# Operand forms of a two-level product moved from VectorE to GpSimd and to an earlier product, in a kernel of attention, Fourier mixing and a channel MLP

## The chip, the core and the metric

The kernel runs on one core of a Trainium2 chip. The metric is the device time of one execution in microseconds (us). The core's engines run side by side, each through its own queue in program order: TensorE (PE; its weight loads are listed apart as PEld), VectorE (DVE), ScalarE (ACT), GpSimd (POOL) and SyncE (SP), which starts the DMA transfers here. They wait for each other by semaphores.

## What is computed

```
# 8 batches, 8 heads, 576 rows, head dimension 64; all fp32
scores = (q @ k.T) / sqrt(64)
scores = where(scores >= max(scores) - tau, scores, -1e9)
attn   = exp(scores - max(scores)); attn = attn / (sum(attn) + 1e-9)
x      = attn @ v                                # heads side by side: (8, 576, 512)
u      = x + real(fft(fft(x, axis=1), axis=2))   # Fourier mixing
un     = (u - mean(u)) / sqrt(var(u) + 1e-6)     # over the 512 channels
out    = u + relu(un @ w_ch1) @ w_ch2            # 512 -> 2048 -> 512
```

## The kernel before

**Steps.** Attention runs in 160 steps, 20 for each batch: four pairs of heads, five steps for each pair. A step computes scores (L440, L446), takes their row maxima on VectorE (L520), exponentials on ScalarE (L526), the threshold and masked sum (L530, L540), the reciprocal of the sum (L385, L388) and the scaling (L549). The result is transposed on TensorE (`pw`, L605; its end rows `pe`, L587) and copied out by ScalarE (L607, L609; `ends`, L593), and is multiplied by the values (`pv`, L636).

**Mixing.** The 576 rows of a batch are folded by symmetry into `f` (L687, L692, L699, L703), one pair of heads at a time; `partial_sums` (L729, L730, then L721 three times, by way of `scaled`) makes sums of the folded halves as soon as enough pairs are there, and `mixing` takes them up in the next batch (L751 to L754 and again L721). Then come small matrix products along the rows (`py`, L766, copied out by ScalarE as `y_e` and `y_o`, L771 and L776) and along the channels (`pa`, L783 and L787; L799 on ScalarE, L803 and L804 on VectorE, L808 and L812 on GpSimd). A row is normalised (`pn`, L858; L863, L864; statistics L869, L870).

**Channel MLP.** The 4608 rows of all batches go through the MLP in groups of 512, group 0 in the plain way and groups 1 to 8 in `two_level`. There each of the two matrix products is made with seven products of half-size blocks in place of eight (a Strassen-Winograd scheme). For the second product this is done on two levels. On the outer level, h (the hidden activations, four quarters a11, a12, a21, a22 in the tile `hs`) gives seven left operands: a11, a12, S1 = a21 + a22, a22, S2 = S1 - a11, a11 - a21 and a12 - S2, numbered 1, 2, 5, 4, 6, 7, 3 in the order in which they are used. I call the seven products by their place in this order, 0 to 6. On the inner level each operand gives seven inner blocks, of which four must be formed: `l2_forms` (L1191) makes two on VectorE and two on GpSimd, of 128x512 each, during the product before. Seven inner products `jn` of four matmuls each (L1398) make up one outer product.

**Rooms.** S1 lies in `s1_tile`. The operands S2, a11 - a21 and a12 - S2 are formed in place by `l1_form` (L1168), each in four pieces of 128x512. S2 is written over S1 before the change; so its pieces stand behind TensorE's reading of S1 in product 2. The room of a11 has had its last reader once a11 - a21 is formed (product 1) and S1 - a11 (products 2 and 3).

**Side jobs.** Which job is issued after which inner product is written out by hand: `at_slots(at, slots, jobs)` (L1321 to L1342) puts jobs at (outer product, inner product), and `slot` (called after the matmuls of each inner product) issues them, so they take their place in the queue of their engine there. Besides operand forms these are the sums over the inner products for each output quarter: `gather` (L1263, five additions on GpSimd) and `finish` (L895, two operations on VectorE, which scale by the row's standard deviation and add to u; L890 takes the reciprocal before the first of them). What is not done within `two_level` goes on in the first product of the next group. The results of the seven products go from PSUM into rows of `w_all`, by ScalarE (L1410) or added by VectorE (L1412, L1418).

**How the two are woven.** `two_level` is a generator that yields after each inner product; `fill` (L1487) advances it within the steps of attention by a budget, and `mix(1)` advances the mixing. TensorE's order is thus the order of the program text. The first products of group 3 run beside the last steps (18 and 19) of a batch and the first of the next. Groups 6 to 8 run with hardly any attention beside them; group 8 is the last (`whole`), where outer products 5 and 6 are plain (L1377).

A next group's first product takes row blocks of the normalised u as its right operand, formed by GpSimd (`t_room`, L1132) in groups 1 to 6 and by VectorE in the last two; its results are taken up by VectorE (L1147) and ScalarE (L1152).

## Time and profile before

| | us |
|---|---|
| median of 3 runs | 1551.99 |
| lowest and highest | 1551.36, 1552.12 |
| profiled execution | 1552.55 |
| its span in the profile | 1550.8 |
| TensorE busy (of the span) | 1523.1 |
| VectorE busy | 1066.9 |
| ScalarE busy | 917.1 |
| GpSimd busy | 776.8 |

The page also gives the granted TensorE clock, 0.999 as a mean. Of the operations that the change touches, the trace has these:

| operation | line | engine | count | median ns of one |
|---|---|---|---|---|
| S2, in four pieces for each group | L1168 | VectorE | 32 | 684 |
| a11 - a21 | L1168 | GpSimd | 32 | 1277 |
| a12 - S2 | L1168 | GpSimd | 32 | 1341 |
| `scaled` of f | L721 | VectorE | 24 | 531 |
| `scaled` of the sums | L721 | VectorE | 8 | 528 |
| `finish` from `w_all` | L895 | VectorE | 64 | 478 |

The outer products of group 3 begin at 778.1, 790.9, 800.1, 810.9, 822.8, 835.1 and 850.6 us of the span. In the windows between them, from product 2 on, VectorE is busy for 10.12, 9.59, 12.16, 11.26 and 9.34 us (the last up to 869.5) and GpSimd for 6.18, 3.97, 7.87, 5.01 and 10.53 us.

A line of the timeline gives the start, the busy time, the engine, the line, the operation, the tile written and those read, shapes, and how many instructions it stands for; in brackets stands how long the engine was idle before it and who ended that. "Busy" is the time from the first to the last of the instructions in the line. In the list of groups, "mean ns" is of one instruction.

### The profile page before, as it was taken

How to read it: one execution, taken by the hardware profiler on the slowest of the kernel's cores; microseconds unless marked ns; L12 is line 12 of the kernel's file. 1: busy time of each engine (PE TensorE's matmuls, PEld its weight loads, DVE VectorE, ACT ScalarE, POOL GpSimd, SP SyncE). 2: the span in 40 equal slices, each digit the busy share in tenths (PEclk: the TensorE clock that was granted, in tenths of full speed). 3: DMA queues.
4: the chain of work that ended last, by engine and by line, in shares of the span. 5: the costliest groups of instructions: out<-in, count | busy, mean ns of one | idle time of the engine just before them, and what ended most of it. 6: DMA issues, size and time to landing. Idle time of an engine off the chain costs nothing.

```text
span 1550.8 us, 27036 instructions
## 1 busy us (share of the span) xinstructions
PE 1523.1 (98%) x9786; PEld 1185.1 (76%) x9786; DVE 1066.9 (69%) x2141; ACT 917.1 (59%) x1921; POOL 776.8 (50%) x964
## 2 busy tenths in 40 slices
PE   8999999999999999999999999999999999999999
PEld 5555555556788777877788778887788778989999
DVE  7987676846779466866588566956687666746546
ACT  6875675655656576656766666666666676232131
POOL 3775553034365643545254724555264626646635
PEclk9999999999999999999999999999999999999999
DMA  6423233465866344634464354635464534646655
GB/s 168 132 59 119 78 92 108 136 204 159 269 200 189 111 150 133 195 102 141 143 186 140 117 159 135 195 93 166 125 191 135 159 117 140 221 163 226 236 198 184
DMA packets 248907, 239.31 MB, mean 154 GB/s; under 512 B 197027, under 2 KB 218533, under 8 KB 228678
## 3 DMA queue, kind: packets, MB, share of 16 engines
q1 hardware_dynamic: 246262, 237.28, 50.1%
q8 instruction: 78, 1.28, 0.3%
q10 hardware_dynamic: 2512, 0.30, 0.1%
q14 instruction: 55, 0.45, 0.1%
HBM read 205.93 MB, written 31.46 MB: 153 GB/s over the span
## 4 chain that ended last, share of the span: by engine, by line
PE 84%; DVE 9%; ACT 3%; DMA 1%; POOL 1%; issue 1%; SPq 0%; ACTq 0%; DVEq 0%; POOLq 0%
PE ph L1210 25%; PE po L1398 18%; PE sc L440 9%; PE pv L636 9%; PE pw L605 7%; PE po L933 4%; PE ph L909 2%; PE sc L446 2%; PE py L766 2%; PE pa L783 1%; PE pe L587 1%; PE pa L787 1%; PE pm L360 1%; PE po L1377 1%; PE pn L858 1%
## 5 line engine op out<-in xcount | busy, mean ns | idle before, releaser
L520 DVE TENSOR_REDUCE neg<-sc 128x1 f32<-128x576 f32 x216 | 154.2, 750 | 113.0 <-PE sc L440 99.6
L526 ACT ACTIVATE e<-sc,neg 128x576 f32<-128x576 f32 x216 | 158.6, 734 | 121.6 <-DVE neg L520 121.5
L1147 DVE TENSOR_TENSOR hs<-ph,hs 128x512 f32<-128x512 f32 (+1 forms) x128 | 105.4, 823 | 168.0 <-PE ph L1210 97.7
L1398 PE MATMUL po<-w,w_all 128*128 128x128 f32 x1728 | 219.4, 276 | 0.3 <-ACT ends L593 0.3
L1398 PEld LDWEIGHTS po<-w,w_all 128*128 128x128 f32 x1728 | 205.0, 192 | 9.4 <-issue 4.0
L1156 POOL TENSOR_TENSOR w<-hs 128x512 f32<-128x512 f32 x32 | 42.1, 1317 | 313.8 <-ACT hs L1152 240.0
L540 DVE SCALAR_TENSOR_TENSOR e<-sc,thr,e 128x576 f32<-128x576 f32 x216 | 168.3, 812 | 20.6 <-ACT thr L530 20.6
L1210 PE MATMUL ph<-u_t,w 128*128 128x256 f32 x768 | 180.9, 382 | 0.5 <-DMA w<-f 0.5
L440 PE MATMUL sc<-kT,qT 64*128 64x288 f32 x1024 | 169.8, 431 | 7.1 <-DVE e L477 6.1
L607 ACT COPY e_t<-pw 128x512 f32<-128x512 f32 x256 | 148.6, 595 | 44.1 <-PE pw L605 42.7
L605 PE MATMUL pw<-ident,e 128*128 128x128 f32 x1152 | 168.8, 273 | 6.0 <-ACT ends L593 1.9
L549 ACT ACTIVATE e<-e,den 128x576 f32<-128x576 f32 x216 | 157.4, 775 | 8.9 <-DVE den L388 8.2
L1210 PEld LDWEIGHTS ph<-u_t,w 128*128 128x128 f32 x768 | 140.9, 190 | 23.6 <-issue 5.3
L1210 PE MATMUL ph<-w_all,w 128*128 128x256 f32 x672 | 157.1, 382 | 1.1 <-DVE w_all L1132 1.0
L605 PEld LDWEIGHTS pw<-ident,e 128*128 128x128 f32 x1152 | 134.8, 141 | 21.9 <-issue 5.6
L1152 ACT ACTIVATE hs<-hs 128x512 f32<-128x512 f32 (+1 forms) x96 | 74.1, 772 | 114.5 <-DVE hs L1147 113.7
L1210 PEld LDWEIGHTS ph<-w_all,w 128*128 128x128 f32 x672 | 123.4, 190 | 23.9 <-issue 4.9
L440 PEld LDWEIGHTS sc<-kT,qT 64*128 64x128 f32 x1024 | 96.3, 187 | 57.1 <-issue 23.7
L1263 POOL TENSOR_TENSOR w_all<-w_all 128x128 f32<-128x128 f32 (+2 forms) x160 | 118.4, 757 | 29.1 <-DVE w_all L1418 20.2
L1398 PE MATMUL po<-w,hs 128*128 128x128 f32 x912 | 120.0, 278 | 0.3 <-ACT ends L593 0.3
L1398 PEld LDWEIGHTS po<-w,hs 128*128 128x128 f32 x912 | 109.9, 192 | 9.9 <-issue 8.0
L593 ACT COPY ends<-pe 128x128 f32<-128x128 f32 (+1 forms) x128 | 38.1, 298 | 58.7 <-PE pe L587 40.1
(227 smaller groups left out, 2945.3 us busy)
## 6 DMA issues: line engine op xcount, KB each, us to landing
w<-f SPq DMA_DIRECT2D x150, 1024.0 KB, 4.9
hs<-in_moe_w_ch_dram SPq DMA_DIRECT2D x23, 512.0 KB, 4.7
q_in<-in_q_dram SPq DMA_DIRECT2D x128, 72.0 KB, 4.3
out_dram<-u SPq DMA_DIRECT2D x36, 256.0 KB, 2.5
k_in<-in_k_dram SPq DMA_DIRECT2D x124, 72.0 KB, 2.4
v_in<-in_v_dram SPq DMA_DIRECT2D x64, 128.0 KB, 5.0
f<-w SPq DMA_DIRECT2D x14, 512.0 KB, 3.3
f<-w SPq DMA_DIRECT2D x7, 1024.0 KB, 4.8
```

What stands on the lines that cost most here:

```text
L440: nc.tensor.matmul(sc[j][:, c, 0:HALF], qT[hp, 128 * t : 128 * t + 128], kT[hp, k0 + HALF * c : k0 + HALF * (c + 1)], start=True, stop=True,)
L520: nc.vector.tensor_reduce(out=neg[:, j : j + 1], in_=sc[j][:, :, 0:HALF], axis=AXIS_XY, op=ALU.max, negate=True,)
L526: nc.scalar.activation(out=ej, in_=sc[j][:, :, 0:HALF], func=ACT.Exp, bias=neg[:, j : j + 1], scale=1.0)
L540: nc.vector.scalar_tensor_tensor(out=ej, in0=sc[j][:, :, 0:HALF], scalar=thr[:, j : j + 1], in1=ej, op0=ALU.is_ge, op1=ALU.mult, accum_out ...
L549: nc.scalar.activation(out=e[:, S * j : S * (j + 1)], in_=e[:, S * j : S * (j + 1)], func=ACT.Copy, scale=den[:, j : j + 1],)
L605: nc.tensor.transpose(pw[:, c, :], e[:, c0 : c0 + 128], ident[:, :])
L607: nc.scalar.copy(e_t[:, 4 * j : 4 * j + 4, qs], pw[:, :, :])
L636: nc.tensor.matmul(pv[64 * j : 64 * j + 64, 0:m], vt[:, 2 * c + j, :], e_t[:, 4 * j + c, 0:m] if c < 4 else ends[:, 0, 0:m], start=(c == 0 ...
L1147: nc.vector.tensor_tensor(out=to, in0=bank, in1=to if other is None else other, op=ALU.add)
L1210: nc.tensor.matmul(bank[:, 256 * q : 256 * q + 256].rearrange("p (two n) -> p two n", two=2), left[:, 256 * c + 128 * q : 256 * c + 128 * ...
L1263: return lambda: eng.tensor_tensor(out=to, in0=to, in1=other, op=ALU.add)
L1398: nc.tensor.matmul(to, lefts[m][j][:, s], right_[:, 128 * s : 128 * (s + 1)], start=jn in (0, 4) and s == 0, stop=s == 3, skip_group_check ...
```

## The change

1. S2 goes into the room of a11 instead of S1's, and GpSimd forms its four pieces in product 2 (after inner products 0, 1, 2 and 4). VectorE did so before, at the end of product 2 and the start of 3.
2. a12 - S2 (operand 3) is formed by GpSimd in product 3 instead of product 4.
3. The gather and the finish of the first output quarter, from `v_11`, move: the gather from product 2 to product 5, the finish from product 4 to product 6, after inner products 3 and 5. In the last group they go to product 4.
4. `partial_sums` starts earlier: L729 and L730 are issued at the end of step 18 instead of in step 19. The L721 of the sums stays in step 19 and the two L721 of f come in step 19 as well, where they came in the first step of the next batch. The last `next(partials)` after the loop goes.

The matmuls, their order and the order in which DMAs are issued are the same.

```diff
-        a = {1: a11, 2: a12, 5: s1_tile[:, :], 4: a22, 6: s1_tile[:, :], 7: a21, 3: a12}
+        a = {1: a11, 2: a12, 5: s1_tile[:, :], 4: a22, 6: a11, 7: a21, 3: a12}
...
         at_slots(1, (1, 2, 4, 6), l1_form(a21, a11, a21, (P, P, P, P)))
-        at_slots(2, (4, 5, 6), l1_form(s1_tile, s1_tile, a11, (V, V, V, V))[0:3])
-        at_slots(3, (0,), l1_form(s1_tile, s1_tile, a11, (V, V, V, V))[3:4])
-        at_slots(4, (1, 2, 4, 6), l1_form(a12, a12, s1_tile, (P, P, P, P)))
-        at_slots(2, (0, 1, 2, 3, 4), gather(P, v_11))
-        at_slots(4, (2, 4), [lambda n=n: finish(0, 0, v_11)[n]() for n in range(2)])
+        at_slots(2, (0, 1, 2, 4), l1_form(a11, s1_tile, a11, (P, P, P, P)))
+        at_slots(3, (2, 4, 5, 6), l1_form(a12, a12, a11, (P, P, P, P)))
+        if whole:
+            at_slots(4, (0, 1, 2, 3, 4), gather(P, v_11))
+            at_slots(4, (5, 6), [lambda n=n: finish(0, 0, v_11)[n]() for n in range(2)])
+        else:
+            at_slots(5, (1, 2, 3, 4, 5), gather(P, v_11))
+            at_slots(6, (3, 5), [lambda n=n: finish(0, 0, v_11)[n]() for n in range(2)])
...
         if i % per_batch == 19:
-            partials = partial_sums(i // per_batch)
-            next(partials)
-        if i % per_batch == 0 and i > 2 * per_batch:
             next(partials)
...
         fill(apart=i % per_batch == 2)
+        if i % per_batch == 18:
+            partials = partial_sums(i // per_batch)
+            next(partials)
...
     while held:
         held.pop(0)()
-    next(partials)
     weights = weights_in_parts(total - 1)
```

## The prediction

> **What bounds the kernel now.** I read the page's busy times first, then the list of what TensorE (PE) waited for in the stretch from 350 us to the end (columns: engine, tile and line that waited, who released it; us in total, times, longest), then the timeline around those waits.

> ```profile
> PE 1523.1 (98%) x9786; PEld 1185.1 (76%) x9786; DVE 1066.9 (69%) x2141; ACT 917.1 (59%) x1921; POOL 776.8 (50%) x964
> ...
> PE 84%; DVE 9%; ACT 3%; DMA 1%; POOL 1%; issue 1%; SPq 0%; ACTq 0%; DVEq 0%; POOLq 0%
> ```

> PE is busy for 98% of the span at a full granted clock. The change touches no matmul and no DMA, so it can win only PE's idle time: 1201.0 - 1187.25 = 13.75 us of the 1201 us after 350 us (where the two-level groups run).

> ```profile
> PE py L766 <- ACT y_e L776: 2.2, 4, 0.7
> ...
> PE pw L605 <- ACT w_all L1410: 1.5, 1, 1.5
> PE pw L605 <- DVE w_all L1418: 1.1, 1, 1.1
> ```

> Three of the four py stalls (839.04, 1008.19, 1177.61; groups 3, 4, 5) and the pw stall of 1.06 (group 2, 665.99) lie at the border of second-level products 4 and 5, counted from 0, where the change works. The stall of 1.52 at 808.58 lies in product 2 of group 3. The five waits on hs L1147, the 0.98 on L1132 and the 0.5 on a DMA lie elsewhere and stay. The timeline of a py stall (start, duration):

> ```profile
> 832.08 0.96 DVE L895 SCALAR_TENSOR_TENSOR u<-w_all,rstd,u 128x256 f32<-128x256 f32 x1
> ...
> 834.62 0.68 DVE L1418 TENSOR_TENSOR w_all<-w_all,po 128x512 f32<-128x512 f32 x1
> ...
> 835.21 0.48 DVE L895 SCALAR_TENSOR_TENSOR u<-w_all,rstd,u 128x256 f32<-128x256 f32 x1
> 835.61 0.55 DVE L1418 TENSOR_TENSOR w_all<-w_all,po 128x384 f32<-128x384 f32 x1
> 836.08 1.42 DVE L520 TENSOR_REDUCE neg<-sc 128x1 f32<-128x576 f32 x2
> ...
> 839.04 0.71 PE L766 MATMUL py<-dim_s,f 128*128 128x128 f32 x4 [0.67 <-ACT y_e L776]
> ```

> VectorE (DVE) has a queue here: both additions of the first output quarter (L895) stand ahead of the score maxima (L520), for which ScalarE's exponentials and then its y_e copy wait; PE's py waits for y_e.

> **Part 1: the first quarter's finish leaves product 4 (gain).** It takes L890 (0.16) and two L895 (0.96 stretched, 0.48) out of DVE's queue: 1.6 us of busy time, about 1.3 by starts. The four forms of operand 3 leave GpSimd (POOL) here too, and with them DVE's waits beside them. Each py stall costs 0.67, or 0.83 from start to start against the usual spacing: 3 x 0.83 = 2.5, gone because 1.3 exceeds 0.83. In group 2 the pw stall, 1.22 + 0.12 by starts, waits for an L1418 behind the same queue; in group 1 the py stall of 0.35. Sum -4.2. Bounds: -5 (neighbouring small stalls go too) and -2.5 (only the py stalls go). I take -4.2: the queue in front is the same in all five.

> **Part 2: the finish comes back in product 6 (loss).** There it precedes this chain of group 3:

> ```profile
> 862.59 0.69 DVE L1418 TENSOR_TENSOR w_all<-w_all,po 128x512 f32<-128x512 f32 x1 [2.52 <-PE po L1398]
> ...
> 865.06 0.46 DVE L803 TENSOR_TENSOR tmp<-pa,tmp 128x289 f32<-128x289 f32 x1
> ...
> 865.60 0.80 POOL L808 TENSOR_TENSOR u_t<-x,tmp 128x289 f32<-128x289 f32 x1 [5.37 <-DVE tmp L803]
> ...
> 873.09 1.41 POOL L1132 TENSOR_TENSOR t_room<-u_t 128x256 f32<-128x256 f32 x2
> ...
> 874.55 0.51 PEld L1210 LDWEIGHTS ph<-t_room,w 128*128 128x128 f32 x3 [0.29 <-POOL t_room L1132]
> ```

> DVE waits for PE (2.52 idle), works in order to L803, and from there POOL runs back to back to the t_room forms of the next group; PE's weight load already waits 0.29 for the second one. In the five groups beside attention PE takes these tiles 0.05 and 0.26 us after they are ready, so the cover is 0.05. The reciprocal and the first L895 now come between L1418 and L803: 0.19 + 0.39, by starts 0.58. All but 0.05 reaches PE: 0.53 x 5 = +2.7. Bounds: 0, if the scheduler's order leaves L803 ahead; +4.5, if both additions stand there (0.39 + 0.58 = 0.97, less 0.05, x 5 = 4.6). I take the one addition that the built order shows ahead of it. The gather (5 POOL adds, 0.73 + 0.46 + 0.46 + 0.90 + 0.72 = 3.3 us) goes to product 5, where POOL is idle for 10.5 of 15.5 us: nothing.

> **Part 3: operand 6 by GpSimd in product 2, partial sums moved (loss).** DVE loses four L1168 (median 684 ns), POOL gains four at a median of 1277 ns: POOL's 6.18 us of the 10.8-us product 2 become 6.18 - 3.3 + 4 x 1.28 = 8.0, so it has room. But the four run back to back from about 800 us, beside this queue of DVE:

> ```profile
> 802.96 0.53 DVE L721 SCALAR_TENSOR_TENSOR sums<-sums,factors,f 128x304 f32<-128x304 f32 x1
> 803.40 0.68 DVE L1191 TENSOR_TENSOR w_all<-hs 128x512 f32<-128x512 f32 x1
> 803.45 1.77 POOL L1191 TENSOR_TENSOR w_all<-hs 128x512 f32<-128x512 f32 x1 [1.32 <-PE po L1398]
> 804.19 1.57 DVE L1191 TENSOR_TENSOR w_all<-w_all,hs 128x512 f32<-128x512 f32 x1
> ...
> 805.68 1.41 DVE L520 TENSOR_REDUCE neg<-sc 128x1 f32<-128x576 f32 x2
> ...
> 806.46 0.74 ACT L526 ACTIVATE e<-sc,neg 128x576 f32<-128x576 f32 x1 [2.42 <-DVE neg L520]
> ...
> 808.58 0.66 PE L605 MATMUL pw<-ident,e 128*128 128x128 f32 x4 [1.52 <-ACT w_all L1410]
> ```

> The second DVE L1191 takes 1.57 instead of 0.68: with POOL at work it is held. Such rows are on record for every DVE operation with both inputs in SBUF (L692 0.34 to 1.37, L895 0.48 to 0.95, L721 0.53 to 1.31); L520, whose input is in PSUM, never stretches. After, this queue holds no L729 and L730 (0.80 by starts; they go to the end of step 18, where DVE idles 1.61 us before L520 at 797.96: nothing), but two more L721 of f (0.88): +0.1. And any of its five operations can meet a running POOL form, against one now: each hold costs 0.9 as in the row above, so 0 to 4 x 0.9 = 3.6 more. I take 2.2, two and a half holds; L520 comes 2.3 us later. ScalarE had idled 2.42 us for it, so all passes through L526 and L1410 to the pw stall: +2.3 in group 3. In group 1 I put +0.8 (0 to 1.0). Groups 2, 4, 5 have 2.1 to 2.5 us of slack between L540 and PE's next scores, the nearest row to a delay of 2.3: 0 to 0.5 each, 0.2 taken. Sum 2.3 + 0.8 + 0.6 = +3.7, from 0 to 3.7 + 1.0 + 1.5 = +6.2. In product 3 DVE loses four L1168: there it had waits on PE anyway, no gain.

> [...]

> **Part 4: operand 3 a product sooner (loss).** The four forms, now in slots 2 to 6 of product 3, run into the folds L687 and L692, which precede the maxima of step 22. Before, it was their other end that was struck:

> ```profile
> 821.02 1.81 DVE L687 TENSOR_TENSOR half<-x 128x287 f32<-128x287 f32 x2
> ...
> 822.76 3.14 DVE L692 TENSOR_TENSOR f<-half 128x143 f32<-128x143 f32 x4
> 823.01 2.73 POOL L1168 TENSOR_TENSOR hs<-hs,w 128x512 f32<-128x512 f32 x2
> ```

> Four L692 took 3.14 where free ones take 4 x 0.34. With the forms earlier, more of the L687 and L692 are held, L520 is 0.1 to 1.4 later, and PE's pw after the ends copy (L593) has a cover of 0.06 us (group 4, 998.28). I put 0.5 in each of groups 3 to 5: +1.5, bounds 0 (the forms only change places) and +3.7.

> Groups 6 to 8 have no attention work. There POOL would need 16 x 1.3 = 21 us in four products of 6.4 (25.6): it fits, and the end is set by PE's last product (L1377, 7.31 us) and two L895. Nothing, though with little room.

> **Sum:** -4.2 + 2.7 + 3.7 + 1.5 = +3.7 on the profiled execution's 1552.55 (span 1550.8 and 1.75 around it), 1556.2. The median shown is 0.56 lower: **1555.6 us**.

> **Rivals.**
> *Cancelling.* Half the holds of parts 3 and 4 fall where DVE would have waited for PE: 3.7 + 1.5 becomes 2.0, sum +0.5, within 1550.5 to 1553.5. For it: POOL idle half the time, slack over 2 us in three groups. Against: the stall at 808.58 has no slack.
> *Faster (the other side).* The holds cost nothing because GpSimd's forms wait for PE slots and so come after DVE's queue, and L803 is not delayed by the finish: only part 1 is left, -4.2 to -2.5, so 1547.8 to 1549.5. It decides once parts 2 to 4 together stay under 1.1. Against: the 0.29 wait on t_room, and operand forms that need no PE result.
> *Holds everywhere.* Parts 3 and 4 at their upper ends and the second addition ahead of L803: -4.2 + 4.6 + 6.2 + 3.7 = +10.3, 1562.3; with only two of the three at their ends 1558.5 to 1560. For it: the stretched rows. Against: the slack of groups 2, 4 and 5.
> *The change does not do what it says:* GpSimd late with operand 6 in the last groups, and PE waits in product 4 there. Its forms are due two products after they are issued; 0.5 to 2 us in three groups, inside the case above.

> **How the numbers follow.** The forecast (1553.5 to 1558.5) 0.45; cancelling 0.20; faster 0.20; holds everywhere 0.15. Faster or slower means by over 0.2% (3.1 us), about what a measurement can tell from none: below 1548.9, above 1555.1. Of the forecast 0.10 lies below 1555.1, of the faster case 0.05 above 1548.9. So faster 0.15, same 0.10 + 0.20 + 0.05 = 0.35, slower 0.35 + 0.15 = 0.50. The range runs from 1549.0, which leaves out about 0.13, to 1560.0, which leaves out 0.07.

> **What would show it.** Part 1: no wait of py on y_e at groups 3 to 5, none of pw on w_all L1418. Part 2: PE's wait for t_room at 0.8 instead of 0.29. Part 3: the pw stall of group 3 near 3.8 instead of 1.52, and DVE's L721 and L1191 there over 1 us each. Part 4: new waits of pw on the ends copy in product 4. If DVE's operations in product 2 keep their lengths, part 3 is wrong and the time falls below 1553.

## The result, and the profile after

The changed kernel takes 1560.93 us (median of 4 runs, 1559.72 to 1562.14), the kernel before beside it 1552.05 us: a ratio of 1.0057, 95% interval 1.0039 to 1.0074. Measured once more, it took 1561.30 us, and the kernel before beside it 1550.73 (1.0065, 1.0052 to 1.0079). So the change costs 8.9 and 10.6 us, where +3.7 was forecast, and its median lies above the range given (to 1560.0).

The page's busy times and chain, after:

```profile
PE 1527.3 (98%) x9786; PEld 1186.2 (76%) x9786; DVE 1061.3 (68%) x2109; ACT 915.9 (59%) x1921; POOL 816.2 (52%) x996
...
PE 81%; DVE 7%; POOL 5%; ACT 3%; issue 2%; DMA 1%; DVEq 0%; POOLq 0%; ACTq 0%
```

VectorE has 32 instructions less and GpSimd 32 more, as the change says. VectorE is 5.6 us less busy and GpSimd 39.4 us more, and GpSimd now takes 5% of the chain instead of 1%. Lines from `plain_product` on stand three lines further down: L1398, L1410, L1412, L1418 are now L1401, L1413, L1415, L1421. What PE waited for from 350 us on:

```profile
PE pw L605 <- ACT w_all L1413: 3.9, 1, 3.9
...
PE ph L1210 <- POOL t_room L1132: 1.5, 3, 0.5
...
PE py L766 <- ACT y_e L776: 0.9, 5, 0.2
PE po L1401 <- ACT ends L597: 0.9, 1, 0.9
PE po L1401 <- DVE w_all L1415: 0.7, 1, 0.7
```

Against the list of before: the py wait is down from 2.2 to 0.9 and the pw wait on L1418 (1.1) is gone, as forecast. The pw wait in group 3 has grown from 1.5 to 3.9, and three waits are new: t_room at the end of product 6, and two in group 1.

Both kernels issue the same 9786 matmuls in the same order. So each can be paired with itself, and its start in the profile after, less its start in the profile before, tells where time is lost. I call this the shift. It is -2.89 us at 350 us, before any changed code (the last section tells why), and +7.49 at the end: the changed code costs 10.4 us. The steps of the shift, in us:

| where | forecast | measured, and its places |
|---|---|---|
| part 1, finish out of product 4 | -4.2 | -2.9: group 2 -1.05, groups 3 to 5 -0.62 each |
| part 2, finish in product 6 | +2.7 | +4.3: 0.86 to 0.88 in each of groups 1 to 5 |
| part 3, product 2 and the sums | +3.7 | +7.6: group 1 2.0; groups 2, 4, 5 0.5 each; group 3 2.4 for the stall and 1.6 after it |
| part 4, operand 3 in product 3 | +1.5 | +0.5 |
| groups 6 to 8 | 0 | +1.3: 0.8 at the start of group 8, 0.4 in its product 4 |
| start of group 3's second product | 0 | -0.35 |

The timeline of group 3, product 2, after:

```profile
799.68 3.74 POOL L1168 TENSOR_TENSOR hs<-w,hs 128x512 f32<-128x512 f32 x3
...
802.25 1.50 DVE L721 SCALAR_TENSOR_TENSOR sums<-sums,factors,f 128x304 f32<-128x304 f32 x1
...
803.68 3.00 DVE L721 SCALAR_TENSOR_TENSOR f<-f,factors 128x304 f32<-128x304 f32 x2
...
804.84 1.50 POOL L1168 TENSOR_TENSOR hs<-w,hs 128x512 f32<-128x512 f32 x1
...
807.99 1.41 DVE L520 TENSOR_REDUCE neg<-sc 128x1 f32<-128x576 f32 x2
...
810.89 0.84 PE L605 MATMUL pw<-ident,e 128*128 128x128 f32 x4 [3.92 <-ACT w_all L1413]
```

Each L721 takes 1.50 where its median before was 0.53, while GpSimd's forms run beside it. The maxima L520 behind them in VectorE's queue come 2.3 us later, and PE stands still for 3.92 us.

### The profile page after: what moved, and what is told of

Its sections match the earlier page's. It is cut to its first block, busy times and chain, and to the rows that moved or that the text cites. A ratio compares the mean times of both kernels' runs of the same rounds, so it can differ in the third digit from the quotient of the medians.

```text
span 1558.3 us, 27012 instructions
## 1 busy us (share of the span) xinstructions
PE 1527.3 (98%) x9786; PEld 1186.2 (76%) x9786; DVE 1061.3 (68%) x2109; ACT 915.9 (59%) x1921; POOL 816.2 (52%) x996
## 3 DMA queue, kind: packets, MB, share of 16 engines
q8 instruction: 78, 1.28, 0.3%
## 4 chain that ended last, share of the span: by engine, by line
PE 81%; DVE 7%; POOL 5%; ACT 3%; issue 2%; DMA 1%; DVEq 0%; POOLq 0%; ACTq 0%
PE ph L1210 23%; PE po L1401 17%; PE pv L636 10%; PE sc L440 9%; PE pw L605 6%; PE po L933 4%; PE ph L909 3%; PE sc L446 2%; PE py L766 2%; POOL u_t L808 1%; POOL u_t L812 1%; PE pe L587 1%; PE pm L360 1%; PE po L1380 1%; ACT e L526 1%
## 5 line engine op out<-in xcount | busy, mean ns | idle before, releaser
L520 DVE TENSOR_REDUCE neg<-sc 128x1 f32<-128x576 f32 x216 | 154.1, 750 | 117.5 <-PE sc L440 108.8
L526 ACT ACTIVATE e<-sc,neg 128x576 f32<-128x576 f32 x216 | 158.7, 734 | 120.4 <-DVE neg L520 120.1
L1401 PE MATMUL po<-w,w_all 128*128 128x128 f32 x1728 | 221.3, 278 | 2.0 <-ACT ends L597 0.9
L1147 DVE TENSOR_TENSOR hs<-ph,hs 128x512 f32<-128x512 f32 (+1 forms) x128 | 105.3, 822 | 166.6 <-PE ph L1210 96.4
L1401 PEld LDWEIGHTS po<-w,w_all 128*128 128x128 f32 x1728 | 206.7, 193 | 11.7 <-issue 4.5
L540 DVE SCALAR_TENSOR_TENSOR e<-sc,thr,e 128x576 f32<-128x576 f32 x216 | 168.2, 811 | 20.4 <-ACT thr L530 20.1
L1210 PE MATMUL ph<-u_t,w 128*128 128x256 f32 x768 | 181.1, 382 | 0.8 <-DMA w<-f 0.5
L605 PE MATMUL pw<-ident,e 128*128 128x128 f32 x1152 | 168.7, 273 | 7.5 <-ACT w_all L1413 3.9
L1210 PEld LDWEIGHTS ph<-u_t,w 128*128 128x128 f32 x768 | 140.9, 190 | 24.4 <-issue 4.6
L1210 PE MATMUL ph<-w_all,w 128*128 128x256 f32 x672 | 157.7, 383 | 1.2 <-DVE w_all L1132 1.0
L605 PEld LDWEIGHTS pw<-ident,e 128*128 128x128 f32 x1152 | 134.9, 141 | 23.5 <-issue 5.6
L1401 PE MATMUL po<-w,hs 128*128 128x128 f32 x1104 | 145.2, 278 | 0.0
L1210 PEld LDWEIGHTS ph<-w_all,w 128*128 128x128 f32 x672 | 123.1, 190 | 25.0 <-issue 4.9
L1401 PEld LDWEIGHTS po<-w,hs 128*128 128x128 f32 x1104 | 132.9, 192 | 11.4 <-issue 9.6
L1191 POOL TENSOR_TENSOR w_all<-hs 128x512 f32<-128x512 f32 x46 | 61.4, 1334 | 60.2 <-PE po L1401 54.8
```

The source lines that it names most:

```text
L520: nc.vector.tensor_reduce(out=neg[:, j : j + 1], in_=sc[j][:, :, 0:HALF], axis=AXIS_XY, op=ALU.max, negate=True,)
L526: nc.scalar.activation(out=ej, in_=sc[j][:, :, 0:HALF], func=ACT.Exp, bias=neg[:, j : j + 1], scale=1.0)
L540: nc.vector.scalar_tensor_tensor(out=ej, in0=sc[j][:, :, 0:HALF], scalar=thr[:, j : j + 1], in1=ej, op0=ALU.is_ge, op1=ALU.mult, accum_out ...
L605: nc.tensor.transpose(pw[:, c, :], e[:, c0 : c0 + 128], ident[:, :])
L1147: nc.vector.tensor_tensor(out=to, in0=bank, in1=to if other is None else other, op=ALU.add)
L1210: nc.tensor.matmul(bank[:, 256 * q : 256 * q + 256].rearrange("p (two n) -> p two n", two=2), left[:, 256 * c + 128 * q : 256 * c + 128 * ...
```

## The experiments

Theory: GpSimd's forms hold VectorE's operations with two SBUF inputs, in product 2 above all, and the finish in product 6 delays t_room. Rivals: the moved sums make the loss of product 2; the operand forms made the py stalls. "Shift" below is that of PE's matmuls against the kernel before, from 350 us to the end, of one profile; the ratio is of the timed runs to those of the kernel before, measured beside them.

| run | median us | kernel before | ratio, interval | shift |
|---|---|---|---|---|
| finish_moved_only | 1553.45 | 1551.17 | 1.0015 (1.0006 to 1.0025) | +2.8 |
| finish_in_hole | 1548.80 | 1551.17 | 0.9983 (0.9974 to 0.9993) | -2.6 |
| sums_moved_only | 1551.53 | 1551.17 | 1.0002 (0.9992 to 1.0011) | +0.9 |
| change_without_sums | 1557.91 | 1551.17 | 1.0049 (1.0031 to 1.0068) | +7.0 |
| s2_by_vector | 1556.17 | 1550.77 | 1.0027 (1.0016 to 1.0038) | +3.5 |
| operand3_late | 1564.68 | 1550.77 | 1.0081 (1.0067 to 1.0096) | +10.6 |
| change_finish_in_gap | 1562.79 | 1550.77 | 1.0069 (1.0055 to 1.0084) | +8.0 |
| best_of_both | 1549.27 | 1550.77 | 0.9985 (0.9976 to 0.9994) | -3.0 |
| operand6_gpsimd_only | 1554.99 | 1550.73 | 1.0027 (1.0015 to 1.0039) | +3.8 |
| change_again | 1561.30 | 1550.73 | 1.0065 (1.0052 to 1.0079) | +11.7 |
| longer_stall_2 | 1554.22 (one) | 1550.73 | | +2.5 |
| longer_stall_4 | 1557.07 (one) | 1550.73 | | +3.9 |

**The finish alone, as in the change.** The kernel before with only the third edit of the change (`gather` and `finish` as in its diff).

> The kernel before with one part alone: gather and finish of the first output quarter in products 5 and 6, as in the change. Theory (three terms, measured between the two profiles by the shift of PE's matmuls after 350 us): the py and pw stalls at the border of products 4 and 5 go, -0.6 in each of groups 3 to 5 and -1.0 in group 2, and the wait for t_room at the end of product 6 grows by 0.86 in each of groups 1 to 5, +4.3: about +1.5 us in all, 1553 to 1554. Rival (the loss in product 6 comes from GpSimd's operand forms and not from the finish): the gain alone, -3 us, 1549.

The shift shows both steps: -0.5 at the py of groups 3 to 5 and -1.0 in group 2, and +0.8 to +0.9 before t_room in groups 1 to 5. Net +2.8 us by the profile and +2.3 by the ratio: the theory's terms, with costs that it had not counted (0.15 to 0.25 at a py in product 5 of groups 3 to 5, 0.4 in group 6, 0.3 at the start of group 8). So the finish with its gather, and not an operand form, makes the loss in product 6; the run with the finish two inner products earlier, below, tells the finish from the gather.

**The finish alone, at the end of product 5.**

```diff
-        at_slots(4, (2, 4), [lambda n=n: finish(0, 0, v_11)[n]() for n in range(2)])
+        if whole:
+            at_slots(4, (2, 4), [lambda n=n: finish(0, 0, v_11)[n]() for n in range(2)])
+        else:
+            at_slots(5, (5, 5), [lambda n=n: finish(0, 0, v_11)[n]() for n in range(2)])
```

> The kernel before with the finish alone moved, to the end of product 5 (after inner product 5), where VectorE has 3.1 us without work in group 3 (846.44 to 849.54); the gather stays in product 2. Theory: the gain at the border of products 4 and 5 without the loss in product 6: -3.3 us, about 1548.7. Rival (the stalls at the border come from the operand forms of GpSimd that stand there): no gain, 1552.

Ratio 0.9983: 2.6 us faster, short of the 3.3 expected. Its timeline in group 3:

```profile
834.13 0.71 PE L766 MATMUL py<-dim_s,f 128*128 128x128 f32 x4 [0.18 <-ACT y_e L776]
...
841.39 0.88 DVE L895 SCALAR_TENSOR_TENSOR u<-w_all,rstd,u 128x256 f32<-128x256 f32 x2
...
844.64 0.56 DVE L1421 TENSOR_TENSOR w_all<-w_all,po 128x384 f32<-128x384 f32 x1 [2.37 <-PE po L1401]
```

The py stall is 0.18 instead of 0.67, and after both additions VectorE still waits 2.37 us for PE: here they lie in time that nobody wanted. The operand forms of product 4 are in their old place in this kernel, so they had not made more than the 0.18 that stays.

**The sums alone.** The kernel before with only the fourth edit.

> The kernel before with the partial sums alone moved, as in the change. Theory (GpSimd's forms of operand 6 hold VectorE): in product 2 of group 3 the longer queue by two L721 is nearly paid by the two operations that left, so the stall of 1.52 at 808.58 grows by less than 0.5; in group 1 L729 stands behind GpSimd's a11 - a21 ahead of the maxima, +0.8. In all +1 us, 1553. Rival (the loss is made by the partial sums): the stall in group 3 grows by 2 us or more, and the time by 4 to 6 us, 1556 to 1558.

Two steps: +0.84 in group 1 and +0.24 on the stall of group 3. The rival (2 us or more in group 3) falls. In the whole time it can't be told from no change.

**The change without the sums.** The changed kernel with the fourth edit undone.

> The changed kernel with the partial sums where they were before. Theory: the stall in group 3 stays over 3 us, and 0.8 us of group 1 come back: about 1560. Rival: most of the 7.5 us lost in product 2 comes back, 1554 to 1556.

The pw stall of group 3 is 3.67 instead of 3.92, so the sums are not its cause: L729 and L730, back in this queue, are held as the L721 of f had been (1.39 and 1.53). The shift is 3.4 us less than the change's. Of this 0.9 is group 1 and 0.25 the stall; 1.6 is that the matmuls after the stall ran at their full rate this time, which I had not expected (the last section has a reason); the rest is small steps.

**Operand 6 by VectorE again.**

```diff
-        at_slots(2, (0, 1, 2, 4), l1_form(a11, s1_tile, a11, (P, P, P, P)))
+        at_slots(2, (4, 5, 6), l1_form(a11, s1_tile, a11, (V, V, V, V))[0:3])
+        at_slots(3, (0,), l1_form(a11, s1_tile, a11, (V, V, V, V))[3:4])
```

> The changed kernel with operand 6 formed by VectorE again, at its old places (product 2 after inner products 4, 5, 6, product 3 after 0), but in the room of a11; all else as changed. Theory (GpSimd's forms in product 2 hold VectorE's queue): the losses of product 2 go, 1.0 in group 1, 0.5 each in groups 2, 4, 5, and in group 3 the stall falls from 3.92 to about 1.75 and the half-rate matmuls after it go; so do 0.4 us at the end, where GpSimd is late in group 8. What stays is the 0.84 of group 1 from the sums. In all 6 us less than the changed kernel, 1553 to 1555. Rival (the longer queue of sums, or the room, makes the loss): within 1.5 us of the changed kernel, above 1556.

The same place as above:

```profile
802.65 0.50 DVE L721 SCALAR_TENSOR_TENSOR sums<-sums,factors,f 128x304 f32<-128x304 f32 x1
...
803.07 0.97 DVE L721 SCALAR_TENSOR_TENSOR f<-f,factors 128x304 f32<-128x304 f32 x2
...
809.13 0.65 PE L605 MATMUL pw<-ident,e 128*128 128x128 f32 x4 [1.76 <-ACT w_all L1414]
```

The very same three operations take 1.5 us instead of 4.5, and the stall is 1.76. The shift falls by 6.9 us against the change; the median, 1556.2, lies above the expected 1553 to 1555 and just inside the rival's "above 1556". But the rival also asked for a time within 1.5 us of the changed kernel, and by the ratios it is 4.6 to 5.9 us below (1.0027 against 1.0057 and 1.0065). VectorE's queue holds the same sums as in the change, and the room is the same: the holds made the loss, not the number of sums or the room.

**Operand 6 by GpSimd alone.** The kernel before with the finish at the end of product 5, and

```diff
+        at_slots(2, (0, 1, 2, 4), l1_form(a11, s1_tile, a11, (P, P, P, P)))
+        at_slots(4, (1, 2, 4, 6), l1_form(a12, a12, a11, (P, P, P, P)))
+        at_slots(3, (0, 1, 2, 3, 4), gather(P, v_11))
```

in place of the old forms and gather (and 6: a11).

> The kernel before with operand 6 alone formed by GpSimd in product 2, in the room of a11; operand 3 in product 4 and the sums as before, the gather in product 3 to make room, the finish at the end of product 5 (the place that gave -3 us). Theory (those forms hold VectorE, whatever else moves): against the finish alone in that place, +1.0 in group 1, 0.5 each in groups 2, 4 and 5, +2.2 in group 3 and 0.4 at the end: 5.1 us more, so +2 us against the kernel before, about 1553, and 1.6 more if matmuls at half rate follow the stall. Rival (the forms cost only together with the moved sums or operand 3): as with the finish alone, 1548 to 1549.

1554.99: against the finish alone the shift grows by 6.4 us, and the steps are those of the change: 1.1 in group 1 (PE waits 0.9 for L597), 0.3 to 0.4 in each of groups 2, 4 and 5, +2.15 on the stall (3.67) and 1.6 after it, 0.7 in the last group; the -0.35 at the start of group 3's second product is here too. Neither the moved sums nor operand 3's move are needed for it, nor the gather's place in product 5.

**Operand 3 late.** The changed kernel with `at_slots(4, (1, 2, 4, 6), l1_form(a12, a12, a11, ...))`.

> The changed kernel with operand 3 formed by GpSimd in product 4 again, from the room of a11. Theory (its move to product 3 is worth little either way): the waits after the ends copy in products 3 and 4 of groups 3 to 5 go, -0.5 us, but the forms again hold VectorE ahead of product 5; if the finish was the only cause of the py stalls there, they stay at 0.17, and the time is within 1 us of the changed kernel, 1557 to 1561. Rival (the forms had made the py stalls): these come back, 3 x 0.5, in groups 3 to 5, and the 1.0 of group 2, so +2 to +2.5 us.

The py waits stay at 0.2, so the forms had not made the stalls. The shift (+10.6) is the change's (+10.4); in the profile the small waits trade places. The median, 1564.68, lies above the theory's range and where the rival had put it, though the intervals overlap. Of the four timed runs the profiled one, at a mean granted clock of 0.998, took 1562.38, and the other three, at 0.995 to 0.997, took 1564.66 to 1565.41; the last section tells what that clock is worth. By the profile part 4 is worth nothing that I could measure.

**The finish in product 6, two inner products earlier.** `at_slots(6, (2, 2), ...)` in the changed kernel.

> The changed kernel with the finish in product 6 after inner product 2, where VectorE has 3.0 us without work in group 3, in place of after 3 and 5. Theory (the finish ahead of the second L803 is what makes PE wait for t_room): the +0.86 in each of groups 1 to 5 goes, and some of the 0.8 lost at the start of group 8: 4.3 us less or a little more, 1553 to 1557. Rival (GpSimd's gather beside it makes t_room late): the wait for t_room stays, within 1 us of the changed kernel.

In groups 1, 3, 4 and 5 the 0.86 goes, as the theory says. In group 2 it doesn't: there both additions come behind the later L1421, still ahead of L803, and PE waits 0.57 more. With 0.5 more in group 6 the shift is 2.4 us less, not 4.3, and the median (1562.79) is no lower than the change's; the last section tells what hides the gain there. Half a miss: one slot is not one place in every group.

**Both together.** The finish at the end of product 5, with L729 and L730 at the end of step 18 from the fourth batch on.

> The kernel before with two edits: the finish at the end of product 5 as in the run with the finish in the hole, and L729 and L730 at the end of step 18 from the fourth batch on, with the three L721 where they were. Theory: the finish gives 3.3 us; the queue ahead of the maxima of product 2 in group 3 is 0.8 shorter, and so is the stall of 1.52 there: -4 us in all, about 1547. Rival (the sums do not move that stall, since GpSimd holds the rest of the queue instead): as with the finish alone, 1548.8.

The stall in group 3 is 1.02 instead of 1.52, and the shift is -3.0 instead of the finish alone's -2.6. (A wait of 0.6 for L1421 at the start of group 8 costs next to nothing: it takes the place of one of 0.50 for a DMA before, and the shift moves by 0.09 there.) The ratio, 0.9985, can't be told from the finish alone's, and the -4 expected was not reached.

**A longer stall by itself.** The kernel before with reductions that nobody reads:

```diff
+        if i == 99:
+            for _ in range(2):   # 4 in the second kernel
+                nc.vector.tensor_reduce(out=filler[:, :], in_=four, axis=AXIS_XY, op=ALU.max)
```

> The kernel before with two further reductions of a constant tile on VectorE (about 0.6 us each, results unused) in step 19 of the fifth batch, ahead of the maxima of product 2 in group 3. It asks what PE does after a stall of about 2.8 us. Theory (matmuls at half rate follow a long stall): at 2.8 us none, only the 1.3 us. Rival (the half rate came from something else in the change): none either; the next run tells.

> As the run before, with four reductions: a stall of about 4 us at the same place, with none of the change's edits. Theory: about 16 matmuls at 213 ns in place of 111.5 follow, 1.6 us on top of the 2.5 us. Rival: all at 111.5, only the 2.5 us.

The stalls came out at 2.57 and 3.40, and after both the matmuls ran at half rate. From 2.57 us I had expected none. The windows of the shorter one (the last numbers are the granted clock, the DMA share and GB/s):

```profile
806.00:808.70 2.70, 0.21 (x2) 0.00 (x0) 2.34 (x5) 2.04 (x5) 1.26 (x1) 1.00 1.17 138
809.20:812.20 3.00, 3.00 (x17) 3.00 (x16) 2.90 (x10) 1.05 (x5) 0.00 (x0) 0.51 0.01 1
813.00:816.00 3.00, 3.00 (x25) 2.29 (x25) 1.59 (x4) 1.66 (x3) 0.00 (x0) 1.00 0.80 317
```

For 3 us after the stall the clock is 0.51, with PE busy all the time, then 1.00. A stall made in another way brings the same 1.6 us, so the stall does it, without the change's edits.

**The change once more.**

> The changed kernel itself once more, beside the runs of this call. Theory: the same stalls in its profile, the 3.9 us in group 3 followed by matmuls at half rate, and 1559 to 1562.

1561.30, and the same stalls. The 3.92 us of group 3 were followed by some 28 matmuls at 213 ns instead of 16: +11.7 in the shift instead of +10.4, and no other place differs by over 0.2.

## Why the prediction was wrong

The direction was right, and each of the four parts shows in the profile, so what failed is mostly the size of terms. By the shift the sum fell short by 6.7 us. The end found is near the rival "holds everywhere" (1558.5 to 1562.3), which had a chance of 0.15, but not by its terms: part 4 took 0.5, not 3.7, and the second addition stands behind L803, not ahead of it. (Two of its three upper ends give 1559.8 to 1560.4 by its own terms, not 1558.5 to 1560.)

- **Part 3, the step that failed most** ("I take 2.2, two and a half holds ... Sum +3.7"). In group 3 the stall grew by 2.40 where 2.3 was forecast, in part by luck, as told below. Missing were three things. The half-rate matmuls behind the stall, 1.6 us: I priced a stall at its length. Group 1: 2.0 instead of 0.8, where all of the queue was held and L729 at the end of step 18, which I had put at "nothing", cost 0.84: there it runs beside GpSimd's a11 - a21 and takes 1.54. And groups 2, 4 and 5 took 0.5, the upper end of "0 to 0.5 each, 0.2 taken": in group 2 the second L540 ahead of PE's scores starts at 639.76 instead of 637.66 us, 2.1 us later. From its end (638.47) to PE's scores (640.24) there had been only 1.77 us, less than the slack of "2.1 to 2.5" that I read.
- **Part 2** ("0.53 x 5 = +2.7"). Measured 0.86 in each group. The first addition and its reciprocal cost 0.68 where 0.58 was forecast (from L1418 to L803 it is 2.47 us before, from L1421 to L803 3.15 after), and nothing of it was covered. The second stands behind L804 and I counted it as harmless; but it runs beside GpSimd's chain to t_room, and an operation of that chain is longer. The L812 before, then the places after:

```profile
866.35 0.70 POOL L812 TENSOR_TENSOR u_t<-x,tmp 128x287 f32<-128x287 f32 x1
...
869.30 0.46 DVE L803 TENSOR_TENSOR tmp<-pa,tmp 128x289 f32<-128x289 f32 x1
...
870.03 0.88 DVE L895 SCALAR_TENSOR_TENSOR u<-w_all,rstd,u 128x256 f32<-128x256 f32 x1
870.59 0.87 POOL L812 TENSOR_TENSOR u_t<-x,tmp 128x287 f32<-128x287 f32 x1
...
877.51 1.41 POOL L1132 TENSOR_TENSOR t_room<-u_t 128x256 f32<-128x256 f32 x2
...
878.28 0.30 PEld L1210 LDWEIGHTS ph<-t_room,w 128*128 128x128 f32 x2 [0.73 <-POOL t_room L1132]
```

  L895 takes 0.88 instead of 0.48, and L812 0.87 instead of 0.70. From the start of L803 to that of L1132 there are 8.21 us, where there were 873.09 - 865.06 = 8.03 before: 0.68 + 0.18 = 0.86. Here operations of both engines grew where they ran side by side, by 0.40 and 0.17.
- **Part 1** (-4.2). -2.9: a wait of 0.17 for y_e stays at each py, and group 1's did not change. I took the whole stall as the gain because the relief of 1.3 exceeded it. The finish in the hole leaves 0.18 too, so something else than the finish sets the rest; what it is stays open. The -0.35 at the start of group 3's second product was not foreseen, and comes and goes among the variants; its cause is open.
- **Part 4** (+1.5). 0.5: two steps of 0.24. The value taken between the bounds of 0 and 3.7 was too high.
- **Groups 6 to 8** ("Nothing, though with little room"). 1.3. In group 7 the finish is held twice by GpSimd and then keeps VectorE from the next group's t_room, and GpSimd is late with the last inner operand of product 4 in group 8:

```profile
1455.21 4.18 DVE L895 SCALAR_TENSOR_TENSOR u<-w_all,rstd,u 128x256 f32<-128x256 f32 x2
...
1539.18 1.16 PE L1401 MATMUL po<-w,w_all 128*128 128x128 f32 x8 [0.16 <-POOL w_all L1191]
```

  "Due two products after they are issued" was a misreading: the inner forms of product 4 are made in product 3, so operand 6 is due one product after it is begun. Put back on VectorE (s2_by_vector), this loss goes.

From 350 us on, in both profiles, L520 and L540, whose `sc` lies in PSUM, take 0.72 to 0.76 and 0.80 to 0.82, beside GpSimd's operations and without them; the L721 of f, with both inputs in SBUF, take from 0.52 to 1.55. In the queue of group 3 the three L721 were held by 1.0 each (1.50 against 0.50, beside forms that take 1.27 alone), the two L1191 not at all (0.68 and 0.69), since GpSimd was idle just then. It is 3 x 1.0 less the one hold of 0.9 before, and 0.1 for the longer queue, 2.2 in VectorE's queue and 2.4 at PE. So the average of two and a half holds met the sum by luck: I did not know which operations would meet a form, and one sign that I had named, L1191 over 1 us, did not come. Holds of 1.0 could be read before: the kernel before has L730 at 1.54 where its median is 0.47, in group 1.

What stays open: the 0.17 at each py, the -0.35 at the start of group 3's second product, and what else than idle time decides on TensorE's clock (last section).

## What to carry to other kernels

Moving an elementwise form from VectorE to GpSimd did not take it out of VectorE's way here: each of the three L721 of group 3, with two SBUF inputs, lost 1.0 us beside forms of 1.27. So look at what stands in VectorE's queue while the moved form runs. Of the four edits one was clearly worth making, in another place: the finish where VectorE waits for PE (-2.6 us). And measure slack from the end of the operation that is delayed, and price a long stall of TensorE with what its clock can do afterwards (here 1.6 us or more after seven of eight stalls of over 2 us in group 3).

## What the runs showed of the hardware

TensorE's clock. In the profile after, around the stall of 3.92 us:

```profile
810.90:814.60 3.70, 3.70 (x19) 3.70 (x20) 2.21 (x7) 1.47 (x7) 0.00 (x0) 0.54 0.12 22
814.60:818.30 3.70, 3.70 (x31) 2.97 (x32) 0.35 (x1) 1.82 (x3) 0.00 (x0) 1.00 0.72 266
```

Matmuls that start 111.5 ns apart start 213 ns apart for some 3.4 us: 16 x (213 - 111.5) = 1.6 us. At this place in the 14 profiles, stalls of 1.0 to 1.76 us (6 profiles) never brought it. Of the eight stalls of 2.57 to 3.92 us seven did, and one of 3.67 did not. The slow stretch began between 0.9 us before the stall's end and 1.1 us after it.

```profile
810.70:814.10 3.40, 3.40 (x31) 3.40 (x32) 2.98 (x9) 2.40 (x9) 0.00 (x0) 1.00 0.28 72
```

Each of the seven others leaves PE without work for 2.37 us or more of one step of the grid. (The stretch of 6.83 us, two steps, had the last 0.89 us of the stall in its first step.)

The starts of the profiles look alike. Each of the 14 profiles has a stall of 1.91 to 1.93 us at 81 to 83 us. In the 7 profiles where PE is without work for 1.82 us or more of one step of the grid, matmuls at half rate follow; in the 7 where it is for at most 1.59, not. Three profiles have slow stretches near 101 and 183 us as well, after stalls of only 1.03 to 1.17 us that are in the other profiles too, while 1.97 us in one step at 808.70 brought none; so the idle time is not all that decides, and what else does stays open. Before 350 us four profiles have no slow stretch (shift -3.4 to -1.8), seven have one (-1.8 to 0, the kernel before among them), two have two (-0.2 and +0.6) and one has three (+1.5), though no run changes the code before it.

It is in the timed runs as well. Beside change_again, the kernel before took 1548.95 to 1550.18 us in the five runs with a mean granted clock of 1.000, and 1553.87 to 1555.15 us in the three with 0.997. The runs of change_finish_in_gap had 0.994 to 0.997, those of the change 0.997 to 0.999, about 0.003 more on average. At a like clock the finish in the gap would then be some 2 to 3 us faster than the change, as it is in the profiles; this is an estimate from these rows. For a difference of 2 us in this kernel, the shift of the matmuls, place by place, tells more than the median of four runs.
